# Attention with normalized queries and keys: three GpSimd shifts a head, whole normalizations, a shorter rsqrt, and another preparation of head 0

## The chip, the cores and the metric

The kernel runs on one core of one Trainium2 chip. The metric is the device time of one execution in microseconds (us); the median over several runs is what is compared. The engines are called by the profile's short names: PE is TensorE (matrix products; PEld its weight loads), DVE is VectorE, ACT is ScalarE, POOL is GpSimd, SP is SyncE, whose queue issues nearly all DMAs.

## The reference

One batch, 32 heads, 2048 positions, head width 20, all in bf16. Queries and keys are divided by their length, the logits are scaled by one number t for each head, and softmax attention follows.

```python
B, H, S, D = 1, 32, 2048, 640
Dh = D // H
def reference(q, k, v, t):
    eps = 1e-6
    qn = q / (jnp.sqrt((q * q).sum(axis=-1, keepdims=True)) + eps)
    kn = k / (jnp.sqrt((k * k).sum(axis=-1, keepdims=True)) + eps)
    logits = jnp.einsum('bhqd,bhkd->bhqk', qn, kn) * t[None, :, None, None]
    attn = _softmax(logits, axis=-1)
    return jnp.einsum('bhqk,bhkd->bhqd', attn, v)
```

Every head has 2048 x 2048 logits, each of which needs an exponential. The head width is only 20, so the exponentials, and not the products, are the bulk of the work.

## The kernel before, in words

**Units.** The logits of one head are cut into 64 units of 128 keys x 512 queries. A unit goes one of two ways to its exponentials.

- The ScalarE way: PE writes waves of two and three units in turn into PSUM (`psA`), ACT takes the exponential of each wave into a ring `p_ring` (L723), and PE multiplies it with the values (`vaug`) into `psO` (L652).
- The VectorE way: four units make a tile. PE writes it in two halves into `psD`. DVE turns each half into 16-bit integers `xt` with one multiply-add (`t1`, L769), whose bits, read as fp16, are a rough exponential. Three shifted copies of the tile (`ss`, one for each of PHASES, an integer addition, L781 on DVE or L787 on POOL) and three scaled copies of the values (`vph`, L484 on POOL) give, with the unshifted tile, four such exponentials whose errors cancel. PE multiplies all four with their values into the same `psO`.

`DVE_TILES` says how many tiles of a head go to DVE: four, and a fifth for `MORE` of the 31 later heads. `KDN` says of how many tiles of a head the last of the three shifts is done by POOL, as two chunks of 512 32-bit integers (with two as the value, `KDN = (2,)`). POOL's ops have a `win`: the planner places them where DVE is in a t1, a transpose or a reduction.

**Preparation of a head.** Loads on SP (k in one DMA, q in four, v in one); then on DVE the squares (`sq`, L503), their sums (L505), and the inverse square root of the sums in small ops on `rs_u`, `rs_a`, `rs_b`, `rs_y`, `rs_r` (L508 to L517): a first guess by integer arithmetic and two Newton steps of three ops each. A last small op multiplies the queries' factors by t (L523). Two heads share one set of small ops from head 3 on. The normalization `qkn` (L534) is done by POOL from head 3 on, in two halves (queries, keys); DVE does it for heads 1 and 2 (L541). SP then issues a DMA transpose of `qkn` into `qkT` (L552), four copies into `qz` and six into `kR` (L392), which bring the keys to other partitions so that products of different units run side by side in PE.

**Head 0** has a way of its own, to start early (`first_head`): DVE normalizes the queries (L574), then the keys (L580); PE transposes both into `psD` (L587), ACT and DVE copy them to `qz` and `qkT` (L596, L601, L604, L606), DVE makes rotated copies of the keys in `kx` (L612), and SP transposes these into `kR` (L614). PE runs a few products on constants (L566, L595)[...]. All 48 ScalarE units of head 0 come before those of head 1.

**After a head's products**, DVE transposes `psO` (L665), takes reciprocals of the sums (L668), and POOL (DVE for the first and last head) divides (L676); SP stores.

**Order.** No engine chooses at run time. Every operation is a task with an engine, an estimated duration, its dependences and a due time. A list scheduler (`list_schedule`) plays the program through with these numbers and writes down one fixed order for each engine; `plan_waits` puts semaphore waits where a dependence crosses engines (and between DVE ops). A DVE op that comes late therefore holds up what stands behind it in every order. Due times come from constants such as LEAD, DLEAD and SPREAD, in units of heads.

Of the kernel before, what the change touches and what calls it, by code (L numbers as in the profile page):

```python
# [22 lines left out]
LOG2E = math.log2(math.e)  # L23
X_MUL = 1024.0 * LOG2E
# [16 lines left out]
class Program:  # L41
# [10 lines left out]
    PE_REST = 6.5  # L52
# [4 lines left out]
    HOLD = {"DVE": 0.0, "PE": 0.1}  # L57
# [48 lines left out]
    def list_schedule(self):  # L106
# [80 lines left out]
        while events or ready["POOL"]:  # L187
# [13 lines left out]
            for e in touched:  # L201
# [5 lines left out]
                if e in soon:  # L207
                    held = [r for r in ready[e] if r[2].name[:2] not in ("t1", "tr") and
                            not (e == "PE" and r[2].name[0] == "q" and r[2].name[2] == "A") and hold(e, now, r[2].dur)]
# [31 lines left out]
                if e == "PE":  # L241
                    kind = t.name[:2]
                    if kind != last_pe[0]:
                        t.end += 0.09
                        self.nsw += 1
# [14 lines left out]
    def plan_waits(self):  # L260
# [4 lines left out]
        for t in self.tasks:  # L265
            for d in t.deps:
                if not d.dma and (d.eng != t.eng or d.eng == "DVE"):
                    d.inc = True
# [14 lines left out]
        for t in allt:  # L283
            kn = known[t.eng]
            need = {}
            for d in t.deps:
                if not d.dma and d.eng == t.eng and d.eng != "DVE":
                    continue
# [27 lines left out]
def bass_standalone__qk_norm__prompt_kernel(  # L316
# [21 lines left out]
    NE = 4  # L338
    GD = 1
    NWARM2 = 5  # L340
    NWARM = 15
    EARLY = 3
    NSOLO = 3
    LEAD = 3.0
    SPREAD = 1.0
    FIRST = -7.0
    DLEAD = 0.8
    PE_MM = 0.23
    MORE = 21
    DVE_TILES = [4 + (h * MORE // 31 > (h - 1) * MORE // 31 if h else 0) for h in range(H)]  # L350
    NDMAX = 6
    NPOOL, FPOOL = True, True
    TTDUR, TTWIN = 0.8, 0.55
    KDN = (2,)
# [3 lines left out]
    with ExitStack() as es:  # L358
        sbuf = lambda name, shape, dt: es.enter_context(nc.sbuf_tensor(name, shape, dt))

        tb16 = sbuf("tb16", [128, H], BF16)
        t_f32 = sbuf("t_f32", [128, H], F32)
# [7 lines left out]
        sq = sbuf("sq", [128, 2 * R, D], BF16)  # L370
# [81 lines left out]
        q0 = []  # L452
# [37 lines left out]
        def add_prep(hs):  # L490
# [9 lines left out]
            sums = []  # L500
            for i, h in enumerate(hs):
                x = qk_sb[h % NB]
                s1 = dv("sq", lambda e, tk, x=x: e.tensor_tensor(sq[:, :, :], x[:, :, :], x[:, :, :], ALU.mult),  # L503
                        0.41, lds[h] + last_sum + (q0[2:] if h == 1 else []))
                sums.append(dv("sum", lambda e, tk, i=i: e.tensor_reduce(  # L505
                    rs["sum"][:, 2 * R * i:2 * R * (i + 1)], sq[:, :, :], AXIS_X, ALU.add), 0.73, [s1] + prep_last[0]))
                last_sum[:] = sums[-1:]
            c = dv("rs", lambda e, tk: e.tensor_scalar(  # L508
                rs["u"][:, 0:w].bitcast(I32), rs["sum"][:, 0:w].bitcast(I32), -0.5, 1597463007.0, ALU.mult, ALU.add),
                0.075 + 0.03 * n, sums)  # L510
            cur = rs["u"]
            for tgt in (rs["y"], rs["r"]):
                c = dv("rs", lambda e, tk, cur=cur: e.tensor_tensor(
                    rs["a"][:, 0:w], cur[:, 0:w], cur[:, 0:w], ALU.mult), 0.07 + 0.03 * n, [c])
                c = dv("rs", lambda e, tk: e.scalar_tensor_tensor(
# [363 lines left out]
```

## Time and profile before

| what | value |
|---|---|
| median of 3 runs | 680.75 us (679.78 to 681.6) |
| profiled execution, its own time | 679.46 us |
| its span, first to last instruction | 677.7 us |
| ACT busy / DVE busy | 664.2 us (98%) / 665.7 us (98%) |
| PE busy / POOL busy | 605.6 us (89%) / 274.7 us (41%) |
| exponentials on ACT (L723) | 581 instructions, 657.4 us |
| t1 on DVE (L769) | 298 instructions, 361.7 us |
| shifts on DVE (L781) / on POOL (L787) | 385, 254.3 us / 124, 154.3 us |
| normalizations on POOL (L534) | 58, 52.4 us |
| first exponential starts / last shift ends | 9.61 us / 673.57 us |

Busy time is the union of an engine's instructions; the mean duration of one is longer than its share, because the end of an instruction overlaps the start of the next. The granted TensorE clock was 0.997 of full speed over the span. The line numbers are those of the kernel before.

### The profile page before, as it was taken

The page shows a single profiled execution, that of the slowest core. Times are in us where ns is not written, and L with a number is a line of the kernel's source. Part 1 is how long each engine was busy: PE and PEld are TensorE (multiplying, and loading weights), DVE is VectorE, ACT ScalarE, POOL GpSimd, SP SyncE. Part 2 cuts the span into 40 slices and gives each one's busy share as a digit, 9 for nine tenths or more (in the row PEclk, how much of TensorE's full clock was granted, in tenths as well). Part 3 has the DMA queues.
Part 4 walks back from the last instruction along what each step waited for, and adds up shares of the span by engine and source line. Part 5 has one row for each costly group of instructions (what it writes and reads, how often), then busy time and mean ns, then how long its engine had stood idle before and what let it go on. Part 6 is the DMA issues. An engine that isn't in the chain of part 4 may idle for free.

```text
span 677.7 us, 14399 instructions
## 1 busy us (share of the span) xinstructions
PE 605.6 (89%) x5862; PEld 165.6 (24%) x5912; DVE 665.7 (98%) x975; ACT 664.2 (98%) x589; POOL 274.7 (41%) x329
## 2 busy tenths in 40 slices
PE   7788899888899998888899988998998999999987
PEld 2122222222222222222222222222222222222222
DVE  8989999999999999999999999999999999999998
ACT  8889999999999999999999999999999999999996
POOL 2144243553424534353443435534245353535311
PEclk9989999999999999999999999999999999999999
DMA  5454515235142351523434143441423424140200
GB/s 63 66 75 73 69 23 89 30 69 61 34 76 32 65 64 42 81 27 80 41 68 66 24 85 33 77 53 37 77 27 77 54 50 73 22 89 6 48 6 11
DMA packets 196722, 36.22 MB, mean 53 GB/s; under 512 B 172592, under 2 KB 196656, under 8 KB 196656
## 3 DMA queue, kind: packets, MB, share of 16 engines
q1 hardware_dynamic: 196512, 35.22, 33.5%
q8 instruction: 46, 0.75, 0.5%
q14 instruction: 20, 0.16, 0.1%
q10 hardware_dynamic: 144, 0.08, 0.1%
HBM read 7.87 MB, written 2.62 MB: 15 GB/s over the span
## 4 chain that ended last, share of the span: by engine, by line
ACT 82%; DVE 13%; PE 1%; DMA 1%; SPq 1%; issue 0%
ACT p_ring L723 82%; DVE xt L769 7%; DVE ss L781 4%; SPq L392 1%; PE psA L633 1%; DVE rs_sum L505 1%; DMA qkT<-qkn 0%; PE psD L633 0%; DVE oT L665 0%; DMA qk_sb<-in_k_dram 0%; DMA kR<-qkT 0%; PE psO L652 0%; DVE sq L503 0%; DVE qz L604 0%; DVE kx L612 0%
## 5 line engine op out<-in xcount | busy, mean ns | idle before, releaser
L723 ACT ACTIVATE p_ring<-psA 128x1024 bf16<-128x1024 f32 x581 | 657.4, 1416 | 6.3 <-PE psA L633 6.2
L769 DVE TENSOR_SCALAR xt<-psD 128x1024 int16<-128x1024 f32 x298 | 361.7, 1214 | 4.9 <-PE psD L633 4.3
L633 PE MATMUL psA<-qz,kR 32*128 32x512 bf16 (+2 forms) x1056 | 224.5, 385 | 45.1 <-ACT p_ring L723 33.4
L781 DVE TENSOR_SCALAR ss<-xt 128x2048 int16<-128x2048 int16 x385 | 254.3, 685 | 1.4
L787 POOL TENSOR_TENSOR ss<-xt,two 128x512 int32<-128x512 int32 x124 | 154.3, 1245 | 141.7 <-DVE ss L781 69.9
L652 PE MATMUL psO<-ss,vph 128*32 128x512 f16 x1788 | 165.2, 385 | 1.5 <-DVE ss L781 1.4
L652 PE MATMUL psO<-p_ring,vaug 128*32 128x512 bf16 x1452 | 137.1, 385 | 0.2 <-ACT p_ring L723 0.2
L633 PE MATMUL psA<-qz,qkT 32*128 32x512 bf16 (+2 forms) x355 | 119.4, 385 | 10.3 <-ACT p_ring L723 6.6
L633 PE MATMUL psD<-qz,kR 64*128 64x512 bf16 (+1 forms) x442 | 120.9, 386 | 6.7 <-DVE xt L769 4.2
L633 PEld LDWEIGHTS psA<-qz,kR 32*128 32x128 bf16 (+2 forms) x1089 | 54.9, 92 | 193.4 <-ACT p_ring L723 188.8
L484 POOL TENSOR_SCALAR vph<-vaug 128x160 f16<-128x160 bf16 (+2 forms) x96 | 40.6, 423 | 143.5 <-DVE ss L781 60.3
L534 POOL TENSOR_TENSOR qkn<-qk_sb,rs_r 128x320 bf16<-128x320 bf16 x58 | 52.4, 905 | 92.0 <-DVE ss L781 67.8
L652 PEld LDWEIGHTS psO<-ss,vph 128*32 128x32 f16 x1788 | 41.8, 94 | 78.1 <-issue 53.0
L652 PE MATMUL psO<-xt,vaug 128*32 128x512 f16 x596 | 59.1, 387 | 0.1
L633 PE MATMUL psD<-qz,qkT 64*128 64x512 bf16 (+1 forms) x145 | 55.2, 386 | 2.8 <-DVE xt L769 1.7
L652 PEld LDWEIGHTS psO<-p_ring,vaug 128*32 128x32 bf16 x1452 | 36.1, 94 | 54.1 <-issue 46.6
L633 PEld LDWEIGHTS psD<-qz,kR 64*128 64x128 bf16 (+1 forms) x447 | 29.2, 94 | 67.8 <-DVE xt L769 48.5
L633 PEld LDWEIGHTS psA<-qz,qkT 32*128 32x128 bf16 (+2 forms) x363 | 29.3, 92 | 58.9 <-ACT p_ring L723 56.3
L676 POOL TENSOR_TENSOR o_stage<-oT,rec 128x320 bf16<-128x320 f32 x30 | 24.6, 821 | 11.9 <-DVE ss L781 10.7
L505 DVE TENSOR_REDUCE rs_sum<-sq 128x32 f32<-128x640 bf16 x32 | 25.7, 803 | 0.1
L665 DVE STREAM_TRANSPOSE oT<-psO 128x512 f32<-128x512 f32 x32 | 22.6, 705 | 1.1 <-PE psO L652 1.1
L652 PEld LDWEIGHTS psO<-xt,vaug 128*32 128x32 bf16 x596 | 15.4, 93 | 31.6 <-issue 26.1
(44 smaller groups left out, 95.8 us busy)
## 6 DMA issues: line engine op xcount, KB each, us to landing
kR<-qkT SPq DMA_DIRECT2D x62, 96.0 KB, 2.1
qz<-qkT SPq DMA_DIRECT2D x124, 32.0 KB, 1.9
kR<-qkT SPq DMA_DIRECT2D x62, 64.0 KB, 2.1
qk_sb<-in_k_dram SPq DMA_DIRECT2D x32, 80.0 KB, 2.4
vaug<-in_v_dram SPq DMA_DIRECT2D x32, 80.0 KB, 3.7
qk_sb<-in_q_dram SPq DMA_DIRECT2D x124, 20.0 KB, 2.5
out_dram<-o_stage SPq DMA_DIRECT2D x31, 80.0 KB, 1.6
kR<-qkT SPq DMA_DIRECT2D x62, 32.0 KB, 1.9
```

The source lines that it names most:

```text
L392: return add(eng, name, lambda e, tk: e.dma_start(dst, src), dur, deps, pri, lat=lat, dma=key)
L484: vsc[h] = [add("POOL", f"vs{h}", lambda e, tk, i=i: e.tensor_scalar(vph[bv][:, i, 0:nd, :], vaug[bv][:, R - nd:R, :], 2.0 ** (-PHASES[i] ...
L505: sums.append(dv("sum", lambda e, tk, i=i: e.tensor_reduce(rs["sum"][:, 2 * R * i:2 * R * (i + 1)], sq[:, :, :], AXIS_X, ALU.add), 0.73, [ ...
L534: u = add("POOL", f"norm{h}", lambda e, tk, x=x, b=b, i=i, j=j: e.tensor_tensor(qkn[b][:, R * j:R * (j + 1), 0:D], x[:, R * j:R * (j + 1), :],
L633: return eng.matmul(dst, lhsT, mov, tile_position=(p0, 0))
L652: last = eng.matmul(psO[32 * g:32 * g + 32, :], w, rhs_of(g), start=start, stop=False, skip_group_check=True, tile_position=(0, 32 * g))
L665: trO[h] = add("DVE", f"tr{h}", lambda e, tk: e.transpose(oT[:, :, :].rearrange("p r d -> p (r d)"), psO[:, :]), 0.63, [lambda: pv_users[h ...
L676: fin[h] = add("POOL" if pool else "DVE", f"fin{h}", lambda e, tk: e.tensor_tensor(st, src, rb, ALU.mult), TTDUR if pool else 0.40, [rc] + ...
L723: act[w] = add("ACT", f"exp{w}", lambda e, tk: e.activation(p_ring[:, p0 * 512:p0 * 512 + n], psA[:, slot * WAVES[0] * 512:slot * WAVES[0] ...
L769: t1_prev[nchunk[0]] = add("DVE", f"t1.{j}.{k}", lambda e, tk, o=o, slot=slot: e.tensor_scalar(xt[sx][:, o:o + W1], psD[:, slot * W1:slot ...
L781: sh.append([dv(f"s{i}.", lambda e, tk, i=i, dst=dst: e.tensor_scalar(dst[:, 0:w], x, float(PHASES[i]), None, ALU.add), 0.533, war)])
L787: u = add("POOL", f"s{i}.{js[0]}.{c}", lambda e, tk, i=i, dst=dst, c=c, n=n: e.tensor_tensor(dst[:, 2 * c:2 * (c + n)].bitcast(I32), xt[sx ...
```

## The change

- `MORE` goes from 21 to 25: four heads more have a fifth DVE tile.
- `KDN` goes from (2,) to (3,): POOL does the last shift of three tiles a head.
- A normalization on POOL is one op over queries and keys (640 elements a partition) instead of two.
- The inverse square root is a guess with another constant and one third-order step: five small ops with the guess instead of seven.
- Head 0: ACT multiplies the queries by t (`xq0`), while DVE works on the inverse root; the keys are normalized in two pieces, before and behind the queries; the first two of their four transposes go to `psA`; ACT's copy of the first half of the keys comes before its copies of the queries; DVE's copies of the queries come before its key rotations.
- `sq` has two buffers, `ss` three instead of four, the planner has some other constants, and it may now hold back PE's products for ACT too while ACT has less than 9 us of planned work ahead. Both are estimates of the planner: no instruction is added for them.

SQPOOL and RSPOOL are False, so `small` makes DVE ops and the squares stay on DVE.

```diff
+RS_MAGIC = 1594963007.0
+RS_K1 = -2.253391575687845
+RS_K0 = 2.282577265641762
...
-    PE_REST = 6.5
+    PE_REST = 4.2
...
-    HOLD = {"DVE": 0.0, "PE": 0.1}
+    HOLDA = 9.0
+    HPE = 0.1
+    HOLD = {"DVE": 0.0, "PE": HPE}
...
-                            not (e == "PE" and r[2].name[0] == "q" and r[2].name[2] == "A") and hold(e, now, r[2].dur)]
+                            not (e == "PE" and r[2].name[0] == "q" and (
+                                r[2].name[2] != "A" or free["ACT"] - now - r[2].dur * 2 - 0.35 < self.HOLDA)) and hold(e, now, r[2].dur)]
...
-    NE = 4
+    NE = 3
...
-    NWARM = 15
+    NWARM = 14
...
-    LEAD = 3.0
+    LEAD = 2.9
...
-    DLEAD = 0.8
+    DLEAD = 0.9
...
-    MORE = 21
+    MORE = 25
...
-    KDN = (2,)
+    KDN = (3,)
...
-                        0.41, lds[h] + last_sum + (q0[2:] if h == 1 else []))
+                          0.41, lds[h] + last_sum[-2:-1] + (q0[2:] if h == 1 else []))]
...
-                rs["u"][:, 0:w].bitcast(I32), rs["sum"][:, 0:w].bitcast(I32), -0.5, 1597463007.0, ALU.mult, ALU.add),
+                rs["u"][:, 0:w].bitcast(I32), rs["sum"][:, 0:w].bitcast(I32), -0.5, RS_MAGIC, ALU.mult, ALU.add),
...
-            for tgt in (rs["y"], rs["r"]):
-                c = dv("rs", lambda e, tk, cur=cur: e.tensor_tensor(
-                    rs["a"][:, 0:w], cur[:, 0:w], cur[:, 0:w], ALU.mult), 0.07 + 0.03 * n, [c])
-                c = dv("rs", lambda e, tk: e.scalar_tensor_tensor(
-                    rs["b"][:, 0:w], rs["a"][:, 0:w], -0.5, rs["sum"][:, 0:w], ALU.mult, ALU.mult), 0.07 + 0.03 * n, [c])
-                c = dv("rs", lambda e, tk, cur=cur, tgt=tgt: e.scalar_tensor_tensor(
-                    tgt[:, 0:w], rs["b"][:, 0:w], 1.5, cur[:, 0:w], ALU.add, ALU.mult), 0.07 + 0.03 * n, [c])
-                cur = tgt
...
+            c = small("rs", lambda e, tk: e.tensor_tensor(rs["a"][:, 0:w], rs["u"][:, 0:w], rs["u"][:, 0:w], ALU.mult), [c])
+            c = small("rs", lambda e, tk: e.tensor_tensor(rs["b"][:, 0:w], rs["a"][:, 0:w], rs["sum"][:, 0:w], ALU.mult), [c])
+            c = small("rs", lambda e, tk: e.scalar_tensor_tensor(
+                rs["y"][:, 0:w], rs["b"][:, 0:w], RS_K1, rs["b"][:, 0:w], ALU.add, ALU.mult), [c])
+            c = small("rs", lambda e, tk: e.scalar_tensor_tensor(
+                rs["r"][:, 0:w], rs["y"][:, 0:w], RS_K0, rs["u"][:, 0:w], ALU.add, ALU.mult), [c])
...
-            c = dv("rs", lambda e, tk: e.tensor_tensor(rq, rq, tq, ALU.mult), 0.07 + 0.03 * n, [c, tcp])
+            if hs[0]:
+                c = small("rs", lambda e, tk: e.tensor_tensor(rq, rq, tq, ALU.mult), [c, tcp])
...
-                    for j in range(2):
+                    m = 2 * R // NCH
+                    for j in range(0, 2 * R, m):
                         u = add("POOL", f"norm{h}", lambda e, tk, x=x, b=b, i=i, j=j: e.tensor_tensor(
-                            qkn[b][:, R * j:R * (j + 1), 0:D], x[:, R * j:R * (j + 1), :],
-                            bc(rs["r"][:, 2 * R * i + R * j:2 * R * i + R * (j + 1)], R), ALU.mult),
-                            TTDUR, [c] + war, due + SPREAD)
-                        u.win = TTWIN
+                            qkn[b][:, j:j + m, 0:D], x[:, j:j + m, :],
+                            bc(rs["r"][:, 2 * R * i + j:2 * R * i + j + m], m), ALU.mult),
+                            m * D * TTRATE + 0.25, [c] + war, due + SPREAD)
+                        u.win = m * D * TTRATE
...
+            qt0 = add("ACT", "qt0", lambda e, tk: e.activation(
+                xq0[:, :, :], x[:, 0:R, :], ACT.Copy, scale=t_f32[:, 0:1]), 0.35, [tcp] + lds[0], -90.84)
+
+            def nk_part(a, b):
+                return add("DVE", "normk0", lambda e, tk: e.tensor_tensor(
+                    kx[:, 32 * a:32 * b].rearrange("p (r w) -> p r w", w=32)[:, :, 0:D],
+                    x[:, R + a:R + b, :], bc(rs["r"][:, R + a:R + b], b - a), ALU.mult), 0.08 + 0.021 * (b - a), [rinv, z_kx], -29)
+            nk1 = nk_part(0, 8)
...
-                x[:, 0:R, :].rearrange("p (g c) d -> p c g d", c=4),
+                xq0[:, :, :].rearrange("p (g c) d -> p c g d", c=4),
...
-                0.4, [rinv, z_qkn[0]], -30)
+                0.4, [rinv, z_qkn[0], qt0], -29)
+            nk = nk_part(8, R)
...
-            tk_ = add("PE", "tk0", lambda e, tk: tmm(e, psD[:, 0:512], kx[:, 0:512]), 0.35, [nk, z_id], -199)
+            tk1 = add("PE", "tk0", lambda e, tk: tmm(e, psA[:, 2048:2560], kx[:, 0:512], 0, 2), 0.15, [nk1, z_id], -201)
+            tk_ = add("PE", "tk0", lambda e, tk: tmm(e, psD[:, 0:512], kx[:, 0:512], 2, 4), 0.2, [nk, z_id], -199)
...
-                qkT[0][:, 512:768], psD[:, 0:256], ACT.Copy), 0.33, [tk_], -89.5)
+                qkT[0][:, 512:768], psA[:, 2048:2304], ACT.Copy), 0.33, [tk1], -90.5)
...
-                qkT[0][:, 768:1024], psD[:, 256:512]), 0.34, [tk_, ka, q0[3]], -24.5)
+                qkT[0][:, 768:1024], psD[:, 256:512]), 0.34, [tk_, ka, q0[2]], -26.25)
...
-                        kv[:, dl, :, g0:g0 + m, :], kv[:, 0, :, s0:s0 + m, :]), 0.15, [nk], -26 if dl > 1 else -26.3))
+                        kv[:, dl, :, g0:g0 + m, :], kv[:, 0, :, s0:s0 + m, :]), 0.22, [nk, q0[2 if dl == 1 else 3]], -26 if dl > 1 else -26.3))
```

## The prediction

> **What bounds the kernel now.** I read the page's busy times first, then the chain that ended last, then the groups, then ScalarE by stages, then the timeline of the one place where ScalarE stands still.
>
> ```profile
> PE 605.6 (89%) x5862; PEld 165.6 (24%) x5912; DVE 665.7 (98%) x975; ACT 664.2 (98%) x589; POOL 274.7 (41%) x329
> ACT 82%; DVE 13%; PE 1%; DMA 1%; SPq 1%; issue 0%
> L723 ACT ACTIVATE p_ring<-psA 128x1024 bf16<-128x1024 f32 x581 | 657.4, 1416 | 6.3 <-PE psA L633 6.2
> L769 DVE TENSOR_SCALAR xt<-psD 128x1024 int16<-128x1024 f32 x298 | 361.7, 1214 | 4.9 <-PE psD L633 4.3
> L781 DVE TENSOR_SCALAR ss<-xt 128x2048 int16<-128x2048 int16 x385 | 254.3, 685 | 1.4
> L787 POOL TENSOR_TENSOR ss<-xt,two 128x512 int32<-128x512 int32 x124 | 154.3, 1245 | 141.7 <-DVE ss L781 69.9
> L534 POOL TENSOR_TENSOR qkn<-qk_sb,rs_r 128x320 bf16<-128x320 bf16 x58 | 52.4, 905 | 92.0 <-DVE ss L781 67.8
> ```
>
> ScalarE and VectorE are both 98% busy: they share the exponentials, and the planner balances them. The chain runs 82% through the exps (L723), 13% through VectorE. GpSimd, at 41%, waits mostly for its place beside VectorE. The exps by stage (stretch, length, busy time and count):
>
> ```profile
> 20.00:30.00 10.00, 10.00 (x10) 1.00 0.46 60
> 30.00:40.00 10.00, 5.14 (x5) 0.83 0.57 90
> 40.00:100.00 60.00, 59.66 (x54) 1.00 0.42 58
> 100.00:650.00 550.00, 549.91 (x488) 1.00 0.33 54
> ```
>
> From 40 us on ScalarE never rests, so there only its own work counts. Between 30 and 40 us it loses half its time. The timeline there, SyncE's queue and ScalarE:
>
> ```profile
> 9.35 3.93 SPq L614 DMA_TRANSPOSE kR<-kx  x3
> ...
> 24.13 1.36 SPq L552 DMA_TRANSPOSE qkT<-qkn  x1
> 27.32 2.50 SPq L392 DMA_DIRECT2D qz<-qkT  x4
> 29.86 3.78 SPq L392 DMA_DIRECT2D kR<-qkT  x6
> ...
> 35.86 2.37 ACT L723 ACTIVATE p_ring<-psA 128x1536 bf16<-128x1536 f32 x2 [4.54 <-PE psA L633]
> ```
>
> Head 0's exps end at 31.3 us. Head 1 can't start before its transpose (issued at 24.13) and the ten copies behind it have landed (35.18 in the chain): 4.54 us of idle time. Before the first exp lie 9.61 us, behind the last one 5.1 us.
>
> **The change part by part.**
>
> *Four tiles from ScalarE to VectorE (MORE 21 to 25).* In the order of the changed kernel there are 306 t1 instead of 298, so 153 VectorE tiles instead of 149, and 1436 ScalarE units of 512 instead of 1452. One unit costs 657.4/1452 = 0.453 us of ScalarE; 16 go: **-7.24 us**. All of it counts, since ScalarE is full from 40 us to its last exp.
>
> *What VectorE then carries.* I use start-to-start distances from the timeline between 40 and 650 us, because the durations overlap: t1 1.14 us with no GpSimd work beside it, a shift 0.61, a small op of the rsqrt 0.14. Added: 8 t1, +9.1. Shifts: the order has 365 on VectorE instead of 385, since GpSimd takes three tiles' last shifts a head instead of two: -12.2. The third-order step makes each of 17 preparations two ops shorter and head 0's three: 37 x 0.14 = -5.2. Sum -8.3 us, about what ScalarE loses. VectorE stays as tight as it was: (665.7 - 8.3)/(677.7 - 8) is again 98%.
>
> *What GpSimd carries.* 188 chunks instead of 124 (+64 x 1.245 = +79.7), and 29 normalizations of 640 elements for 58 of 320. Chunks of 512 took 1.03 us at the least, the 320-element ones 0.72: 1.6 ns an element and 0.2 us fixed, so an estimated 1.25 us for the whole one, 36 us for 52. GpSimd ends near 340 us, half the span: no bound by its busy time. [...] In the trace a chunk issued beside a shift stretches until the next t1 and then runs under it:
>
> ```profile
> 311.04 1.41 POOL L787 TENSOR_TENSOR ss<-xt,two 128x512 int32<-128x512 int32 x1 [1.52 <-DVE ss L781]
> ...
> 311.48 1.22 DVE L769 TENSOR_SCALAR xt<-psD 128x1024 int16<-128x1024 f32 x1
> 312.61 0.48 DVE L503 TENSOR_TENSOR sq<-qk_sb 128x640 bf16<-128x640 bf16 x1
> ```
>
> The square starts on time. Of 278 t1 between 40 and 650 us, 214 had GpSimd work beside them, and their mean distance was 1.159 us against 1.142 for the rest: 0.017 us for each. [...] If each added chunk blocked a shift for its 1.04 us, VectorE would get +67 us. [...] So the cost hangs on whether windows are left: 306 t1, 32 transposes and 32 reductions against 188 + 29 + 30 long GpSimd ops. They are, but fewer. Bounds: nothing (a gain from fewer normalization pieces is excluded by 0.017 x 29) to 64 x 0.13 = 8 us, if a chunk overran by the 0.1 us that VectorE's dependent ops wait anyway. A whole normalization, 1.25 us against t1's 1.14, overruns by 0.1 to 0.3 us unless issued under the shift before: 0 to 9 us for 29. The nearest rows, chunk and half normalization beside t1, say little: 1.5 us in sum, of which the 12 us of VectorE's idle time hide part. I take **+0.6 us**.
>
> *Head 0 and the restart.* In the order, VectorE's way to head 1's normalization now holds four t1 and three shifts instead of five and four, and two rsqrt ops fewer (-1.14 - 0.61 - 0.3). Head 0 itself gains three ops of 0.22, and its PSUM copies no longer stand behind five key copies, but its keys are normalized in two pieces. Head 1's normalization, done at 21.83 before, is done near 19.7. SyncE decides then: its queue ran without a pause to 24.13. Ahead of the transpose one load has moved behind it, and one q load has moved ahead of the three key transposes (all 0.65 us ones, but the one that stood behind took 1.32). 9.35 + 0.65 + 3.93, and 10.74 - 1.32 - 0.65 of loads, put the transpose at 22.7: 1.4 us earlier. The load behind it hides in the transpose's 3.17 us; the copies follow unchanged. So exps restart at 34.5: **-1.4 us**. Bounds: -3.0 (11 loads at 0.65 each, none held up) and 0 (the queue held up as long as before). Head 0's first exp gains 0.9 us by my sum (8.7 instead of 9.61), but that only lengthens the same stall.
>
> *At nothing:* the query scale on ScalarE, done near 5.2 us under VectorE's rsqrt, which ends at 5.65 (if t lands late, 1 us of the first exp, hidden by the stall); TensorE's 48 more value products, 12 groups of 0.23 us, under 72 us of idle time; three shift buffers instead of four (662 us of them over 153 tiles: one comes each 4.3 us, so 13 us for its products to be done); ScalarE's products held back for at most 0.1 us, beside exps already queued; one warm-up product less, GpSimd's smaller vph set and the planner's other constants. The tail ends in the same row of ops, t1 and three shifts. If the shift buffers' cover were gone, a VectorE shift would wait for TensorE, at some 0.4 us a time.
>
> **Sum.** 677.7 - 7.24 - 1.4 + 0.6 = 669.7 us of span. Around the span lie 679.46 - 677.7 = 1.76 us: 671.4 for such an execution, which stood 1.29 us below the median of 680.75. On the median's scale: 672.7 us.
>
> **The rivals.**
> 1. *VectorE takes ScalarE's place.* Windows run short, GpSimd ops begin late[...]. For it: VectorE is 98% full both times and is 13% of the chain. Against: 0.017 us a t1. At 64 x 0.06 us the sum loses 3.8: 676.5.
> 2. *The start gives more*: loads at 0.65 each, so -3.0[...]: 670.5. For it: queue items of 1.3 to 1.5 us looked held up. Against: the held ones are moved, not gone.
> 3. [...] The place is the shift (or square) after each t1 with a chunk or whole normalization under it. With the 8.3 us that VectorE sheds used up, 8.3/64 = 0.13 us an added chunk is the break-even with VectorE's old path. At 0.2 us (fixed part of a chunk, issued when t1 begins rather than before) plus 0.1 us for each normalization: -8.3 - 1.4 + 12.8 + 2.9 = +6.0, so 686.8. Against: the trace has such late starts (1.04 us ones at 308.48 and 314.02) with no late shift behind.
> 4. *The change doesn't move the bound*: stalls of 0.1 us a chunk; 680.
>
> **How the numbers follow.** The sum as it stands 0.62 (alone 670.3 to 674.8), rival 1 0.19, rival 2 0.09, rival 4 0.04, rival 3 0.06. A measurement of this kernel tells about 0.3% (2.0 us) from no change, so faster is below 678.7: 0.90; same 0.04; slower 0.06. The range takes in rival 2's centre and most of rival 1: 669.2 to 677.7.
>
> **What would show it.** Right: 574 or so exps with 650 us busy, ScalarE full from about 40 us on; restart near 34.5 us; VectorE's busy time near 658; t1's distance with GpSimd beside it below 1.18 us; shifts still 0.61. Wrong: ScalarE's idle time waiting for TensorE psA (6.2 us now) growing by several us spread over the run, a chain with VectorE well above 13%, shifts above 0.65 us behind GpSimd ops, or the transpose still issued at 24 us.

## The result and the profile after

The changed kernel takes 671.91 us (median of 4 runs, 671.04 to 672.15) where the kernel before, beside it, takes 680.26 us (679.41 to 681.6). The ratio is 0.9873 [0.9854, 0.9893]: 1.3% faster. The profiled execution took 671.9 us, with a span of 670.2 us (677.7 before).

The busy times, the shares of the chain that ended last, and the groups of the page after, to be laid beside those of before:

```profile
PE 614.8 (92%) x5959; PEld 167.2 (25%) x5959; DVE 655.9 (98%) x927; ACT 657.3 (98%) x584; POOL 350.0 (52%) x364
ACT 88%; DVE 7%; PE 3%; SPq 1%; DMA 1%; issue 1%
L757 ACT ACTIVATE p_ring<-psA 128x1024 bf16<-128x1024 f32 (+1 forms) x575 | 650.1, 1373 | 7.0 <-PE psA L667 7.0
L803 DVE TENSOR_SCALAR xt<-psD 128x1024 int16<-128x1024 f32 x306 | 371.5, 1214 | 7.4 <-PE psD L667 6.5
L821 POOL TENSOR_TENSOR ss<-xt,two 128x512 int32<-128x512 int32 x188 | 234.6, 1248 | 161.4 <-DVE ss L815 80.9
L815 DVE TENSOR_SCALAR ss<-xt 128x2048 int16<-128x2048 int16 x365 | 242.1, 683 | 1.2
L562 POOL TENSOR_TENSOR qkn<-qk_sb,rs_r 128x640 bf16<-128x640 bf16 x29 | 46.8, 1615 | 34.2 <-DVE ss L815 24.2
```

ACT's exponentials went from 657.4 to 650.1 us. DVE got 9.8 us of t1 more and 12.2 us of shifts less, and is at 98% again. POOL took the work over and still has half the span free. The chain moved further to ACT. The exponentials by stretch (start and end, length, busy time and count, granted TensorE clock, DMA share, GB/s):

```profile
20.00:30.00 10.00, 9.98 (x10) 1.00 0.44 60
30.00:40.00 10.00, 3.82 (x3) 0.67 0.62 93
40.00:100.00 60.00, 59.55 (x54) 1.00 0.36 53
100.00:640.00 540.00, 539.63 (x478) 1.00 0.34 55
```

From 40 us to the end ACT is as full as before. Between 30 and 40 us it got less done than before, 3.82 us instead of 5.14, at a mean clock of 0.67 instead of 0.83. The timeline there, SP's queue, ACT, and PE:

```profile
23.18 1.36 SPq L580 DMA_TRANSPOSE qkT<-qkn  x1
26.36 2.49 SPq L403 DMA_DIRECT2D qz<-qkT  x4
28.89 3.77 SPq L403 DMA_DIRECT2D kR<-qkT  x6
...
8.62 21.36 ACT L757 ACTIVATE p_ring<-psA 128x1024 bf16<-128x1024 f32 x19
35.32 2.37 ACT L757 ACTIVATE p_ring<-psA 128x1536 bf16<-128x1536 f32 x2 [5.34 <-PE psA L667]
38.11 1.45 ACT L757 ACTIVATE p_ring<-psA 128x1536 bf16<-128x1536 f32 x1 [0.42 <-PE psA L667]
40.45 5.54 ACT L757 ACTIVATE p_ring<-psA 128x1024 bf16<-128x1024 f32 x5 [0.89 <-PE psA L667]
...
34.25 0.60 PE L667 MATMUL psA<-qz,kR 64*128 64x512 bf16 x1 [2.81 <-DMA kR<-qkT]
34.26 0.60 PE L667 MATMUL psA<-qz,qkT 64*128 64x512 bf16 x1
34.65 1.60 PE L667 MATMUL psA<-qz,kR 64*128 64x512 bf16 x3
```

In the kernel before, the first product and ACT's next two waits were:

```profile
35.22 0.39 PE L633 MATMUL psA<-qz,kR 64*128 64x512 bf16 x1 [2.08 <-DMA kR<-qkT]
...
38.44 1.45 ACT L723 ACTIVATE p_ring<-psA 128x1536 bf16<-128x1536 f32 x1 [0.21 <-PE psA L633]
40.34 5.54 ACT L723 ACTIVATE p_ring<-psA 128x1024 bf16<-128x1024 f32 x5 [0.45 <-PE psA L633]
```

Head 1's transpose leaves SP 0.95 us earlier and its first product starts 0.97 us earlier. But the first exponential follows 1.07 us behind that product, not 0.64 as before, because a product takes 0.60 us where it took 0.39. ACT then stands twice more, waiting for PE, for about twice as long as before (0.42 and 0.89 us, not 0.21 and 0.45). The kernels have the same first 22 exponentials; by the 23rd the gain of the start is gone:

| us | before | after | difference |
|---|---|---|---|
| transpose of head 1 issued | 24.13 | 23.18 | -0.95 |
| first product of head 1 | 35.22 | 34.25 | -0.97 |
| 20th exponential starts (the restart) | 35.86 | 35.32 | -0.54 |
| 23rd exponential starts | 40.34 | 40.45 | +0.11 |
| 23rd exponential to the end of the last one | 632.22 | 625.30 | -6.92 |
| end of the last exponential to the end of the span | 5.16 | 4.40 | -0.76 |
| span | 677.72 | 670.15 | -7.57 |

So between these two executions the whole gain lies in ACT's long full stretch and in the tail. In the tail DVE's last shift ended 1.01 us behind the last exponential before, and 0.26 us now; behind the later of the two come another 4.1 us in both kernels.

The clock in these traces is either 1.00 or 0.50; 0.83 and 0.67 are means. Cut where it changes, PE's stretches are these (columns as above, with PE's busy time), first in the kernel before, then in the changed one:

```profile
29.45:32.86 3.41, 1.99 (x25) 1.00 0.31 77
32.86:36.27 3.41, 1.33 (x10) 1.00 0.65 130
36.27:39.69 3.42, 3.23 (x12) 0.50 0.70 62
...
30.00:33.41 3.41, 0.80 (x8) 1.00 0.38 92
33.41:36.83 3.42, 2.58 (x7) 0.50 0.94 126
36.83:40.24 3.41, 3.41 (x12) 0.50 0.49 55
```

Around the restart PE ran at half rate for 3.41 us before, and for twice that after. In each of the fourteen traces the changes of the clock lie whole multiples of 3.413 us apart, and the first of them comes 4.20 to 7.02 us after the first instruction (6.11 us in the changed kernel, whose products on constants at the start follow each other at 0.43 us up to 5.79 us and at 0.22 us from 6.17 on). So the clock changed by slots of that length in these traces, and where they fall differs from trace to trace. The mean clocks of the other executions fit this (an estimate: one slot at half rate, 3.41 us of 670, lowers the mean over the span by 0.0025), but they don't count the slots at the restart alone: in the trace of after the clock is 0.50 again from 668.29 us to the end, behind the last product. Of the changed kernel's four executions the one at 0.997 took 671.04 us, those at 0.994 and 0.995 took 671.90 to 672.15. Of 44 executions of the kernel before, measured beside the runs below, the 22 at 0.995 or less have a median of 680.86 us, the 16 at 0.997 one of 679.69. The profiled execution of before was one of the latter, that of after one of the former. So the rows from the restart to the 23rd exponential compare unlike executions. Like with like the kernels differ by 8.65 us (679.69 and 671.04) or 8.93 us (680.86 and the other three's median of 671.93), as far as so few executions tell, where these two differ by 7.56. How much of the difference is the restart's isn't shown, since there is no trace of the kernel before with two such slots.

### The profile page after: what moved, and what is told of

It is laid out like the page before. It is cut to its first block, busy times and chain, and to the rows that moved or that the text cites. A ratio compares the mean times of both kernels' runs of the same rounds, so it can differ in the third digit from the quotient of the medians.

```text
span 670.2 us, 14522 instructions
## 1 busy us (share of the span) xinstructions
PE 614.8 (92%) x5959; PEld 167.2 (25%) x5959; DVE 655.9 (98%) x927; ACT 657.3 (98%) x584; POOL 350.0 (52%) x364
## 3 DMA queue, kind: packets, MB, share of 16 engines
q1 hardware_dynamic: 196512, 35.22, 33.7%
## 4 chain that ended last, share of the span: by engine, by line
ACT 88%; DVE 7%; PE 3%; SPq 1%; DMA 1%; issue 1%
ACT p_ring L757 88%; DVE xt L803 3%; DVE ss L815 2%; PE psA L667 1%; PE psO L594 1%; SPq L403 1%; PE psO L686 1%; DMA qkT<-qkn 0%; PE psD L667 0%; DMA kR<-qkT 0%; DVE rs_sum L529 0%; DVE sq L527 0%; DVE qz L638 0%; DVE oT L699 0%; DVE kx L646 0%
## 5 line engine op out<-in xcount | busy, mean ns | idle before, releaser
L757 ACT ACTIVATE p_ring<-psA 128x1024 bf16<-128x1024 f32 (+1 forms) x575 | 650.1, 1373 | 7.0 <-PE psA L667 7.0
L803 DVE TENSOR_SCALAR xt<-psD 128x1024 int16<-128x1024 f32 x306 | 371.5, 1214 | 7.4 <-PE psD L667 6.5
L821 POOL TENSOR_TENSOR ss<-xt,two 128x512 int32<-128x512 int32 x188 | 234.6, 1248 | 161.4 <-DVE ss L815 80.9
L667 PE MATMUL psA<-qz,kR 32*128 32x512 bf16 (+2 forms) x1077 | 236.8, 386 | 33.6 <-ACT p_ring L757 25.8
L815 DVE TENSOR_SCALAR ss<-xt 128x2048 int16<-128x2048 int16 x365 | 242.1, 683 | 1.2
L686 PE MATMUL psO<-ss,vph 128*32 128x512 f16 x1836 | 171.6, 385 | 0.9 <-DVE ss L815 0.9
L667 PE MATMUL psA<-qz,qkT 64*128 64x512 bf16 (+2 forms) x359 | 121.9, 386 | 10.9 <-ACT p_ring L757 9.4
L667 PE MATMUL psD<-qz,kR 64*128 64x512 bf16 (+1 forms) x459 | 126.1, 386 | 3.9 <-DVE xt L803 2.2
L562 POOL TENSOR_TENSOR qkn<-qk_sb,rs_r 128x640 bf16<-128x640 bf16 x29 | 46.8, 1615 | 34.2 <-DVE ss L815 24.2
L667 PEld LDWEIGHTS psA<-qz,qkT 64*128 64x128 bf16 (+2 forms) x359 | 29.2, 92 | 58.2 <-ACT p_ring L757 56.7
L686 PEld LDWEIGHTS psO<-xt,vaug 128*32 128x32 bf16 x612 | 15.8, 93 | 34.1 <-issue 26.8
```

The costliest lines, as they stand in the source:

```text
L562: u = add("POOL", f"norm{h}", lambda e, tk, x=x, b=b, i=i, j=j: e.tensor_tensor(qkn[b][:, j:j + m, 0:D], x[:, j:j + m, :], bc(rs["r"][:, 2 ...
L667: return eng.matmul(dst, lhsT, mov, tile_position=(p0, 0))
L686: last = eng.matmul(psO[32 * g:32 * g + 32, :], w, rhs_of(g), start=start, stop=False, skip_group_check=True, tile_position=(0, 32 * g))
L757: act[w] = add("ACT", f"exp{w}", lambda e, tk: e.activation(p_ring[:, p0 * 512:p0 * 512 + n], psA[:, slot * WAVES[0] * 512:slot * WAVES[0] ...
L803: t1_prev[nchunk[0]] = add("DVE", f"t1.{j}.{k}", lambda e, tk, o=o, slot=slot: e.tensor_scalar(xt[sx][:, o:o + W1], psD[:, slot * W1:slot ...
L815: sh.append([dv(f"s{i}.", lambda e, tk, i=i, dst=dst: e.tensor_scalar(dst[:, 0:w], x, float(PHASES[i]), None, ALU.add), 0.533, war)])
```

## Experiments

The theory was that of the prediction: ACT sets the time, and gets 16 units less; the rest of the change makes DVE room for these units; POOL's added work is nearly free, since it is issued where DVE is in a t1. The rivals were that DVE has room anyway (then `MORE` alone would do), that POOL's ops slow DVE, and that the start brings the gain. That the planner's new constants bring it, without the tiles, is ruled out by the trace of before: ACT idles 0.09 us between its 23rd and its last exponential there, so no other order of the same work could have shortened that stretch. Kernels 1 to 8 and 10 below are planned anew by the list scheduler, so their whole order differs a little; 9, 11 and 12 keep the order of the changed kernel but for the place named. Lines of code are those of the changed kernel, unless before is named.

**1. The tiles alone, in the kernel before** (e1_before_more25).

```diff
-    MORE = 21
+    MORE = 25
```

> The kernel before with MORE 25 alone: four tiles move from ScalarE to VectorE, and nothing else is taken from VectorE. Theory A (both engines are bounds, the other edits pay for the move): VectorE gets 8 t1 (+9.1 us) and 12 shifts (+7.3), 16 us more than it had room for, ScalarE loses 7.24 us. The end follows VectorE: 12 to 17 us slower than before, 692 to 698 us, with ScalarE idle more than 15 us in waits for TensorE psA spread over the run. Theory B (ScalarE alone is the bound, VectorE has room): 673 us.

703.19 us, ratio to before 1.0335 [1.0319, 1.035]. The chain and the exponentials of its page:

```profile
ACT 66%; DVE 23%; PE 8%; DMA 1%; issue 1%; SPq 1%
L723 ACT ACTIVATE p_ring<-psA 128x1024 bf16<-128x1024 f32 (+1 forms) x575 | 652.0, 1378 | 22.0 <-PE psA L633 19.1
```

ACT has the fewer exponentials, but idles 22 us for them; DVE is busy 683.9 us, 18.2 more than before, and its last shift ends 22.7 us later. DVE has no room of its own: the tiles alone cost 3.3%. The time lies above what was expected of the theory (692 to 698).

**2. All of the change but the tiles** (e2_after_more21).

```diff
-    MORE = 25
+    MORE = 21
```

> The changed kernel with MORE 21 again: the relief of VectorE stays, ScalarE has its 1452 units back. Theory A (ScalarE's 16 units are the whole steady gain): exps 657.4 us busy, 7.2 us more than after, so 678.5 to 679.5 us, with VectorE idle 15 us more than in after. Theory B (VectorE was what bound, and its relief is the gain): about 672 us or less, because VectorE loses another 16 us.

678.5 us, 0.9973 [0.9961, 0.9985]. Its busy times and chain:

```profile
PE 626.6 (93%) x5911; PEld 170.7 (25%) x5911; DVE 644.3 (95%) x907; ACT 664.3 (98%) x590; POOL 343.8 (51%) x364
ACT 92%; DVE 3%; PE 2%; SPq 1%; DMA 1%; issue 0%; ACTq 0%
...
662.36 1.90 DVE L815 TENSOR_SCALAR ss<-xt 128x2048 int16<-128x2048 int16 x3
672.88 0.72 DVE L699 STREAM_TRANSPOSE oT<-psO 128x512 f32<-128x512 f32 x1 [8.62 <-PE psO L686]
```

The relief alone is worth 0.3%: DVE falls to 644.3 us and stands 8.62 us at the end, waiting for what ACT still has to do. Runs 1 and 2 together carry the verdict: each half alone brings next to nothing or costs 22 us; both together bring 8.4 us.

**3. POOL's third shift back to DVE** (e4_after_kdn2).

```diff
-    KDN = (3,)
+    KDN = (2,)
```

> The changed kernel with KDN (2,): GpSimd does two tiles' last shifts a head, 32 shifts go back to VectorE, 19.5 us at 0.61. Theory A (VectorE has no room, GpSimd's third tile pays for the move from ScalarE): VectorE busy about 675 us, time 690 to 696 us. Theory B [...]: t1 and shift distances fall, and the time is below 680 us.

687.69 us, 1.0106 [1.0092, 1.012], a little less than the 690 to 696 expected. DVE is busy 673.6 us, 17.7 more than after (32 shifts of 0.61 us are 19.5), and its last shift ends 15.4 us later, 12.3 us behind the last exponential; DVE's share of the chain is 40%. The difference of 2.3 us came out of DVE's idle time between 45 and 640 us (4.8 to 2.5). The third shift on POOL is what makes most of the room for the tiles; 15.8 us is well above what a new plan alone cost in run 10.

**4. The old inverse root** (e7_after_old_rsqrt): two Newton steps and the old guess.

```diff
-                rs["u"][:, 0:w].bitcast(I32), rs["sum"][:, 0:w].bitcast(I32), -0.5, RS_MAGIC, ALU.mult, ALU.add),
+                rs["u"][:, 0:w].bitcast(I32), rs["sum"][:, 0:w].bitcast(I32), -0.5, 1597463007.0, ALU.mult, ALU.add),
...
+            cur = rs["u"]
+            for tgt in (rs["y"], rs["r"]):
+                c = dv("rs", lambda e, tk, cur=cur: e.tensor_tensor(
+                    rs["a"][:, 0:w], cur[:, 0:w], cur[:, 0:w], ALU.mult), 0.07 + 0.03 * n, [c])
...
```

> The changed kernel with the two Newton steps and the old guess: two small ops more for each preparation, 36 ops of 0.14 us, 5.0 us on VectorE. Theory A (VectorE has no room): 4 to 8 us slower than after, 676 to 680 us. Theory B (small ops fill gaps in which VectorE waits anyway): within 1.5 us of after, since VectorE idles 14 us in all.

677.88 us, 0.9965 [0.9953, 0.9977]; DVE busy 660.1 us, 4.2 more than after, ACT idle 5.1 us between 40 and 640 us (0.8 after). The time fits the theory, but run 10 will show that a new plan of the same work can cost as much. Shown is the 4.2 us of work, not that it alone makes the 6 us.

**5. The normalization in two pieces** (e3_after_norm_halves).

```diff
-    NCH = 1
+    NCH = 2
```

> The changed kernel with each GpSimd normalization in two ops of 320 elements again. Theory A (the whole op pays by leaving windows for 29 more chunks; pieces push GpSimd's work out of its windows): GpSimd busy about 356 us, chunks late, shifts stretched, 1 to 6 us slower than after, 673 to 678 us. Theory B (windows are not short): within 1.5 us of after. A new plan goes with it, so a difference below 5 us with VectorE's mean distances unchanged speaks for the plan and not for the pieces.

677.5 us, 0.9964 [0.9951, 0.9977]. POOL's 58 pieces take 950 ns each. With POOL beside it, a t1 is followed by the next start at 1.163 us in the mean (1.150 after), a shift at 0.604 (0.602). These distances contain DVE's waits; DVE idles 9.1 us between 45 and 640 us instead of 4.8, and of the t1 with no wait behind them the distance is 1.133 us, after 1.132. So the pieces don't slow DVE's instructions. Whether they delay heads or the new plan is a worse one, this run can't tell: it is inconclusive.

**6. POOL's chunks anywhere** (e6_after_chunks_any_time): the planner no longer seeks a t1 to put them under.

```diff
-                    u.win = 0.02 + n * PRATE
+                    u.win = 0.0
```

> The changed kernel with the window taken from GpSimd's shift chunks: they are issued as soon as their tile is there, beside whatever VectorE does[...]. Theory A ([...]the placing under t1 is what makes the third shift cheap): a VectorE shift behind a chunk stretches by 0.2 to 1.0 us, mean distance of shifts with GpSimd beside them 0.7 us or more instead of 0.60, VectorE's path longer by 20 to 80 us, 690 to 750 us. Theory B (the engines share without loss): distances unchanged and time within 5 us of after.

758.23 us, 1.1162 [1.1141, 1.1183]. The shifts of its page, and the timeline of one of them:

```profile
L815 DVE TENSOR_SCALAR ss<-xt 128x2048 int16<-128x2048 int16 x365 | 293.7, 829 | 2.0
...
314.44 2.54 POOL L821 TENSOR_TENSOR ss<-xt,two 128x512 int32<-128x512 int32 x2 [2.76 <-DVE xt L803]
...
316.14 1.39 DVE L815 TENSOR_SCALAR ss<-xt 128x2048 int16<-128x2048 int16 x1
317.45 0.81 DVE L529 TENSOR_REDUCE rs_sum<-sq 128x32 f32<-128x640 bf16 x1
```

The shift at 316.14 ends at 317.53, 0.55 us after the second chunk (316.98), as if it had stood until then. The 165 shifts with POOL beside them are followed at 0.87 us in the mean and 1.46 at most, the other 133 at 0.61. So shifts do stretch beside POOL's chunks when these are not placed, as rival 3 feared: the shifts are busy 293.7 us instead of 242.1, 51.6 of the 86 us that this kernel is slower than the changed one. The rest can't be put down to such meetings, since the plan is another one too: behind one t1 DVE waited 6.0 us for PE's products.

**7. Head 0 as before** (e8_after_old_head0): the keys normalized in one piece behind the queries, t put into the factors by DVE, and the copies in the old order.

```diff
-            nk1 = nk_part(0, 8)
...
-                xq0[:, :, :].rearrange("p (g c) d -> p c g d", c=4),
+                x[:, 0:R, :].rearrange("p (g c) d -> p c g d", c=4),
...
-            nk = nk_part(8, R)
+            nk = add("DVE", "normk0", lambda e, tk: e.tensor_tensor(
```

> The changed kernel with head 0 prepared as before: t by VectorE, keys in one piece behind the queries, key rotations ahead of the PSUM copies. Theory A (the earlier first exp only lengthens the stall before head 1): first exp 0.6 to 1.0 us later than 8.62, the stall shorter by as much, restart within 0.8 us of 35.3, time within 0.8 us of after. Theory B (head 0's preparation shortens the run by what its first exp gains): 0.7 to 1.0 us slower than after, 672.6 to 672.9 us.

672.78 us, 0.9891 [0.9877, 0.9904], an interval that overlaps the changed kernel's. The first exponential starts at 8.55 us, not later than in the changed kernel (8.62), so the expectation of a later start missed. But the edit does not bring the old order back: in this plan two key rotations stand ahead of DVE's copies of the queries, five in the kernel before. The copies start at 7.29 us here, 7.35 after, 8.35 before, and the earlier first exponential goes with them. The parallel preparation is not needed for it. The shorter root alone isn't the cause either: run 4, with the old root, starts at 8.60. A single execution tells this to about 0.5 us only; the same start took 8.41 to 9.06 us in runs 9, 11 and 12. Head 1's transpose leaves at 24.66 instead of 23.18 and the restart is at 36.80 instead of 35.32. There the new preparation pays up to 1.5 us, as far as neither the new plan nor such scatter (23.62 for the same order in run 9) has a share in it, and 0.9 us of the span are left of that at the end.

**8. Products on constants ahead of the restart, planned** (e5_after_warm_stall): 16 of them, which enter no result, as tasks of the planner.

```diff
+            if w == 19:
+                for i in range(NWARM3):
+                    stall.append(add("PE", "warm", lambda e, tk: e.matmul(
+                        psA[:, 1024:1536], ones[:, 0:128], ones[:, :], start=True, stop=True), PE_MM, [act[17]], 1.5))
+            if w in (19, 20):
+                deps += stall
```

> The changed kernel with 16 products of constants on TensorE between head 0's last products and head 1's first, in a part of psA that is free then. Theory A (the 0.97 us by which head 1's keys land earlier is lost to TensorE's clock, which falls to 0.67 in 30 to 40 us): granted clock there 0.9 or more, products of head 1 at 0.39 instead of 0.60 us, exps back at 34.9 instead of 35.32 us, and the idle time behind the restart 0.2 to 0.7 instead of 1.31 us; in all 0.8 to 1.3 us less than after: 670.6 to 671.1 us. Theory B (the clock is not the cause, the products wait for landings): restart at 35.3, 671.9 us. Theory C (the filling products run past the landing): restart up to 1 us later.

680.27 us, 0.9997 [0.9989, 1.0005]: missed by every theory. The clock was 1.00 between 30 and 40 us, and the 23rd exponential came at 39.49 us instead of 40.45 although the restart was 1 us later. But the tasks changed the plan of all engines: ACT idled 4.8 us between 40 and 640 us, DVE 9.2, and its last shift ended at 673.90. Planned tasks can't settle a question of 1 us here.

**9. Products on constants ahead of the restart, order kept** (e9_after_warm_fixed_order): 12 such products put into PE's finished order.

```diff
         prog.schedule()
+        qk = restart[0]
+        at = prog.order["PE"].index(qk)
+        for i in range(NWARM3):
+            u = add("PE", "warm", lambda e, tk: e.matmul(
+                psA[:, 1024:1536], ones[:, 0:128], ones[:, :], start=True, stop=True), PE_MM, [act[17]])
+            u.seq, u.start, u.end = len(prog.tasks) - 1, qk.start, qk.start
+            prog.order["PE"].insert(at + i, u)
```

> The changed kernel in its own order of instructions, with 12 products of constants put into TensorE's order behind the planner's work, between head 0's last product and head 1's first; the orders of the other engines are those of after. Theory A (the clock at the restart costs): granted clock in 30 to 40 us above 0.9, head 1's first products at 0.39 us instead of 0.60, from restart to the fourth exp behind it 3.2 to 3.6 us instead of 5.13, so 1.3 to 2.0 us less than after: 669.9 to 670.6 us. Theory B (the earlier attempt's 8 us came from filling TensorE, not from the new plan): 678 to 681 us.

670.76 us, 0.986 [0.9845, 0.9874]. The exponentials of the stretch and the timeline of PE and ACT:

```profile
30.00:40.00 10.00, 4.96 (x6) 1.00 0.55 90
...
31.78 2.76 PE L865 MATMUL psA<-ones 128*128 128x512 bf16 x12
34.78 0.39 PE L668 MATMUL psA<-qz,kR 64*128 64x512 bf16 x1 [0.24 <-DMA kR<-qkT]
...
35.42 10.49 ACT L761 ACTIVATE p_ring<-psA 128x1536 bf16<-128x1536 f32 x9 [5.04 <-PE psA L668]
```

The copies landed 0.5 us later in this execution, and still the 23rd exponential came at 39.00 us, 1.45 us earlier: the clock is 1.00, a product takes 0.39 us, and ACT doesn't stand again behind the restart. From the first product of head 1 to the 23rd exponential it is 4.22 us here, 5.12 before and 6.20 after. The span is 668.73 us, 1.42 less than after. All four executions have a mean clock of 0.999 or 1.000, where none of the changed kernel's has more than 0.997. The intervals of the two ratios overlap; it is the clock, the place in the profile and the size, the same at the 23rd exponential and at the end, that show the cause.

**10. The same instructions in another plan** (e10_after_old_leads).

```diff
-    LEAD = 2.9
+    LEAD = 3.0
...
-    DLEAD = 0.9
+    DLEAD = 0.8
```

> The changed kernel with two of the planner's constants as before, LEAD 3.0 and DLEAD 0.8: the same instructions in another order. Theory A (any new plan of the same work can lose several us, because a plan in which VectorE falls behind is not caught up): between 2 and 9 us slower than after, with VectorE's idle time above 7 us between 45 and 640 us. Theory B (the constants matter little, and what made the first filled kernel slow is the filling): within 1.5 us of 671.9.

677.38 us, 0.9955 [0.9941, 0.9969]. Its chain, and DVE's end:

```profile
ACT 45%; DVE 45%; PE 7%; issue 1%; SPq 1%; DMA 1%; ACTq 0%
...
668.35 1.22 DVE L803 TENSOR_SCALAR xt<-psD 128x1024 int16<-128x1024 f32 x1
669.60 1.90 DVE L815 TENSOR_SCALAR ss<-xt 128x2048 int16<-128x2048 int16 x3
```

ACT's last exponential ends at 665.98 us, as after (665.75). DVE, with the same 306 t1 and 365 shifts, ends at 671.50, 5.5 us later. With both engines at 98%, two due-time constants decide whether DVE ends with ACT or behind it. This is the yardstick for runs 4 and 5. It also says how much of the change hangs on them: with the old values the change brings 0.45%, not 1.3%.

**11. Head 1's transpose ahead of head 4's loads** (e11_after_transpose_first), in SP's finished order.

```diff
         prog.schedule()
+        sp = prog.order["SP"]
+        at, k4 = sp.index(trn[1]), sp.index(lds[4][0])
+        behind = sp[k4:at]
+        sp[k4:at + 1] = [trn[1]] + behind
```

> The changed kernel in its own order, but in SyncE's queue head 1's transpose stands ahead of head 4's k load and three q loads, which now go behind it. The other engines' orders are those of after. Theory A (SyncE's queue, not the normalization, sets when head 1 starts; the normalization is done at 19.51 and the transpose was issued at 23.18): transpose near 20.6, last copy landed near 31.7 instead of 34.21, TensorE idle for less than 1 us and its clock kept, restart at 32.5 instead of 35.32, fourth exp behind it near 36 instead of 40.45; time 2.5 to 4.5 us less than after, 667.4 to 669.4. Theory B (VectorE's work binds behind the restart, so that an earlier one is given back): the fourth exp earlier, but ScalarE idle by as much more between 40 and 640 us, and time within 1 us of after. Theory C (head 4's later loads hold up its squares): VectorE waits near 31 us, restart gain under 1 us.

670.33 us, 0.9861 [0.9845, 0.9877], with all four runs (669.94 to 670.67) below the changed kernel's four, which were not measured beside it. SP's queue and ACT:

```profile
20.50 1.36 SPq L580 DMA_TRANSPOSE qkT<-qkn  x1
21.91 0.57 SPq L403 DMA_DIRECT2D qk_sb<-in_k_dram  x1
22.53 2.65 SPq L403 DMA_DIRECT2D qk_sb<-in_q_dram  x4
25.22 2.53 SPq L403 DMA_DIRECT2D qz<-qkT  x4
27.80 3.77 SPq L403 DMA_DIRECT2D kR<-qkT  x6
...
33.80 17.33 ACT L757 ACTIVATE p_ring<-psA 128x1536 bf16<-128x1536 f32 x15 [3.38 <-PE psA L667]
```

The restart is at 33.80 us, 1.5 earlier, at a clock of 1.00; the 30th exponential starts 2.98 us earlier, the last one ends 1.95 us earlier. About 1 us is given back on the way, so that the time misses what was expected (667.4 to 669.4) by about 1 us. The mean clock of the other three executions is 0.997, so PE was not at full rate throughout in them; where is not shown, since there is no trace of them. As a ratio to before this kernel, run 9 and the changed kernel can't be told apart (0.9861, 0.986, 0.9873, with intervals that overlap); what is shown is the earlier restart.

**12. The same, with two of head 4's loads behind the copies** (e12_after_three_loads).

```diff
+        last = lds[4][-2:]
...
+        at = sp.index(rot[1][-1]) + 1
+        sp[at:at] = last
```

> The kernel with head 1's transpose first, and only three of head 4's five loads between the transpose and its copies; the last two q loads go behind the copies. Theory A (what is left of the stall is still worth its length): copies issued at 23.8 instead of 25.2, last landing near 31.8 instead of 33.1, restart near 32.5 instead of 33.80, time 0.8 to 1.4 us less than that kernel: 669.0 to 669.5 us. Theory B (VectorE's preparation of heads 3 and 4, which stands ahead of head 1's first t1, binds now): its squares wait for the late loads, head 1's first t1 stays at 35 us or later, ScalarE idles after the restart, time within 0.5 us of 670.3 us or above.

672.24 us, 0.9875 [0.9853, 0.9897]. DVE, PE and ACT:

```profile
33.83 0.49 DVE L527 TENSOR_TENSOR sq<-qk_sb 128x640 bf16<-128x640 bf16 x1 [2.64 <-DMA qk_sb<-in_q_dram]
...
38.46 1.03 PE L667 MATMUL psD<-qz,kR 128*128 128x512 bf16 x2 [3.46 <-DVE xt L803]
...
40.39 10.15 ACT L757 ACTIVATE p_ring<-psA 128x1024 bf16<-128x1024 f32 x9 [4.11 <-PE psA L667]
```

The restart comes at 32.57 us, another 1.2 earlier. But head 4's squares stand in DVE's fixed order, and wait 2.64 us for the late loads; PE's products for `psD`, which stand ahead of those for ACT, wait 3.46 us for the t1 behind them, and ACT stops for 4.11 us. The stall was moved, not removed.

## Why the prediction was right, and where it wasn't

The sum gave 669.7 us of span and 672.7 us of median; 670.15 and 671.91 were measured. The main terms were right; that the sum came so close is in part luck, since the restart missed and other terms made up for most of it.

- *Four tiles from ACT, -7.24 us*: right. The exponentials took 7.3 us less, and run 2, which takes the tiles away, gives 6.6 us back.
- *What DVE carries, -8.3 us*: right in the main. DVE is busy 9.8 us less; the shifts gave the -12.2 of the prediction, the t1 rows +9.8 instead of +9.1, and what is left, the small ops in the main, -7.4 instead of -5.2. Runs 1 and 3 show that this relief is a condition and not a margin.
- *POOL's ops beside DVE's, +0.6 us* (rival 2 counted nothing): right in size. ACT idles 0.28 us more between the 23rd and the last exponential than before, whatever its cause. The distance of a t1 with POOL beside it is 1.150 us (252 of them), without 1.146 (37); a shift is followed at 0.60 us with POOL and 0.61 without. The 0.017 us a t1 that the prediction read in the trace of before were DVE's waits and not POOL: of the t1 there with no wait behind them, the 179 with POOL beside them have a distance of 1.131 us, the other 60 one of 1.135. Rival 3, a slower kernel through DVE's shifts, fails since POOL's op is placed under a t1; run 6 shows what a shift costs that meets a chunk (0.87 us in the mean, against 0.61). Why a t1 bears POOL's op beside it and a shift doesn't is not shown: the prediction had the 0.017 us to go by, and the rest was its author's estimate.
- *POOL near 340 us*: 350.0. A whole normalization took 1.27 us at the least, the prediction's 1.25, but 1.615 us in the mean. The two of 1.27 were issued while DVE was in a transpose out of PSUM; the 26 that were issued in a shift took 1.63 to 1.65, as if they had stood until the shift was done and the waiting were recorded as busy. No cost of it shows in DVE's distances (a shift is followed at 0.60 us with POOL beside it, 0.61 without).
- *Head 0 and the restart, -1.4 us*: **the step that failed**; at the 23rd exponential it is +0.11 between the profiled executions. Two things were missed. The transpose left at 23.18 us, not 22.7: the loads between the key transposes and it took 9.20 us, not the 8.77 that were carried over from before. That is 0.45 us, with a little from the key transposes. The rest, 1.06 us, was lost to PE's clock. The prediction took what comes behind the copies as unchanged; it shows the 0.83 in the row of before, and doesn't price it. At half rate for two slots instead of one, the way from the first product to the 23rd exponential took 6.20 us instead of 5.12 (4.22 at full rate, run 9). By the times of the other executions this difference may well be the draw of the two profiled ones, as the section on the result says. What sets PE to half rate is not shown. The slot ahead of half rate was not empty: PE was busy 1.33 of 3.41 us in it before, with a longest gap of 2.08 us, and 0.80 us after. Nor does the length of the gap alone decide: 2.81 us after went with two slots at half rate, 3.24 us in run 10 and 3.27 in run 4 with one (a mean clock of 0.83 between 30 and 40 us in both).
- *The first exponential at 8.7 us, which only lengthens the stall*: 8.62, and the stall grew from 4.54 to 5.34 us. Of the reasons given, the one that the trace bears out is that the copies no longer stand behind five key rotations; the keys in two pieces are not needed for it (run 7).
- *The tail at nothing*: -0.76 us, as DVE's last shift now ends closer to the last exponential. This and the 0.3 us by which the term for POOL's ops was too high make up for two thirds of the 1.51 us that the restart lost; the rest is the half microsecond by which the span was predicted too short.
- *The planner's other constants at nothing*: wrong as a reason. Run 10 puts two of them back and loses 5.5 us. That the new ones cost nothing here was the plan's outcome and could not be read from the instructions; here the prediction was lucky.
- *The step from the profiled execution to the median, +1.29 us*: it didn't carry over. The profiled execution took 671.9 us, the median 671.91. By the clocks, the profiled execution of before was one of those at 0.997, which were 1.17 us quicker in the median than those at 0.995 or less; that of after, at 0.994, was not. So the median was predicted 0.8 us too high, although the span was predicted about half a microsecond too short.

What stays open: how much of the losses of runs 4 and 5 is their own work and how much their plan; how much of the start's gain is left between executions with the same number of slots at half rate; and what the new planner constants would do to the tiles alone (run 1).

## What to carry to other kernels

Where two engines are full, relief of one is worth little and load on it costs dearly (here 0.3% and 3.3%); the gain comes from the trade of both in one change, and each must be priced against its own full stretch. At a stall, read the clock column of the stretch and not only the wait: what comes behind the wait can run slower too (here 0.60 us a product instead of 0.39), and 12 products on constants in the gap gave it back here (run 9). Before two profiles are laid side by side at such a place, compare their clocks with those of the other executions: the difference may be one of executions and not of kernels. In a statically planned kernel test a small question by an edit of the finished order, since a new plan of the same work can move the time by more than most edits (5.5 us in run 10).

## What the runs showed of the hardware that was not expected

- PE's clock was halved for whole slots of 3.413 us, whose place differs from trace to trace. Around a gap of 2.81 us it was halved for two slots (the changed kernel), around one of 2.08 us for one slot (before); in the former the first products behind the gap took 0.60 us, in the latter 0.39. With 12 products of 0.23 us (2.76/12) in the gap the clock was 1.00 between 30 and 40 us (run 9).
- Around the restart a DMA transpose `qkT` holds SP's queue for 1.31 to 1.36 us and a load of head 3 or 4 for 0.57 to 1.4 us (the changed kernel and run 11), so the order in that queue alone moved a head's start: by 2.7 us for its transpose and 1.5 us for its first exponential (run 11).
- A normalization on POOL was recorded with 1.27 us where it was issued beside a transpose out of PSUM, and with 1.63 to 1.65 where it was issued in a shift (the changed kernel). If the difference is waiting, as it looks, POOL's busy share overstates its work: by an estimated 10 us for 26 of them (26 x 0.37).
